# A new order and start of the attention head, GpSimd reciprocals, and a split end in a fused attention and two-MoE kernel

## The chip, the cores and the metric

The kernel runs on one core of one Trainium2 chip. The metric is the device time of one execution in microseconds (us). A core has TensorE (PE, with its weight loads PEld), VectorE (DVE), ScalarE (ACT), GpSimd (POOL) and SyncE (SP), which here issues DMAs. Each engine works through its own queue in order.

## The reference

Window attention (each token sees itself and the 63 before it) is followed by two pairs of dense layers: one with a squared ReLU, one with a rational function.

```python
B, H, S, D = 4, 8, 576, 64
scores = scale * np.matmul(q, k.transpose(0, 1, 3, 2))
mask = (rel >= 0) & (rel < 64)
scores = np.where(mask, scores, -1000000000.0)
attn = np.exp(scores - np.max(scores, axis=-1, keepdims=True))
attn = attn / (np.sum(attn, axis=-1, keepdims=True) + 1e-09)
x = np.matmul(attn, v)                      # to (2304, 512)
h = x @ w_in1; x = (np.maximum(h, 0) ** 2) @ w_out1          # d_ff 2048
h = x @ w_in2
g = (a0 + a1*h + a2*h**2 + a3*h**3) / (1 + |b0|*|h| + |b1|*h**2 + 1e-6)
out = g @ w_out2
```

All arrays are float32. The dense products are made of three products of rounded parts (high by high, high by low, low by high), so each operand is split into a high and a low part before it is used.

## The kernel before

The 2304 tokens are cut into 18 sub-blocks of 128 and five blocks of 512 or less. Attention of a sub-block `i` consists of slots: `q` and `k` (transpose on TensorE, copy out of PSUM to qT and kT), `s` (score products for two groups of 64 queries, `gl` 0 and 1, then `softmax`), `p` (transpose of the probabilities, one for each group, and a copy), `x` (product with v, then `split_x` into xh and xl). For sub-blocks 1 to 3 `y` makes a part of the product with v early. For sub-block 0, `Q`, `K` and `S` are halves of `q`, `k` and `s`, each for half of the heads.

Sub-blocks 0 to 3 (`i < NS0`) form the head: nothing dense can run before their x is there. The list `begin` (L1445) gives the order of their slots, and so the due time of each: n times 30000/32 for entry n. From then on the dense products `h` (L923 for the first one, L933 after it) and `acc` (L950) run, with the attention of later sub-blocks between them. Weights come as two-word numbers: a load, a decode (ScalarE L457, VectorE L459 and L462), a high part (ScalarE L492) and a low part (VectorE L493). At the end the second pair of layers runs (`product` L1301, `outs` L1336), and `evac2` copies the last rows out and stores them. The last 128 rows are made in two halves (L1322), copied (L1392) and stored (L1393) separately.

The order on every engine is fixed when the program is built. `Plan.run` is a list scheduler: it takes the item that can start first by the plan's own durations, at equal starts the one with the earliest due time, and each engine then runs its items in that order. A due time is carried back from user to producer: the user's due time, less the producer's duration, less 150 ns. A copy may name two engines ("act" and "dve"), and the plan picks one. Loads are items of a single DMA engine in the plan; a load of `size` bytes counts `size/360*slow` ns, and lands by the plan `LANDS` ns later, a list that is used up load by load. All of them are issued from SP (L345). PSUM has eight banks; the list `banks` (L569) gives the bank of each of the first slots.

`softmax` (L757): `top` on VectorE adds the mask and takes the row maximum (nm), `exp` on ScalarE gives the exponentials and their sums (su), `norm` on VectorE (L790, L791) makes the reciprocals of the sums (rs), and `mul` multiplies, in the head on GpSimd (L794), later on VectorE. There are two softmaxes in each sub-block, so eight in the head, each with four maxima, four exponentials, one `norm` and one `mul`. `warm_up` (L1437) is six products of `ident` by itself ahead of the first transposes; `ident` and `mask` are made by GpSimd at the start.

For sub-block 0 the first 64 queries have no earlier keys. The kernel before keeps their keys in columns 64 to 127 of the scores, masks columns 0 to 63, and loads the first 64 tokens of v once more to the upper 64 partitions (`load_v`, L423) so that the product with v can use rows 64 to 127.

Of the kernel before, what the change touches and what calls it, by code (L numbers as in the profile page):

```python
# [15 lines left out]
NEG = -1.0e30  # L16
# [139 lines left out]
def window_attention__moe_relu2__moe_rational_kernel(  # L156
# [54 lines left out]
    SMALL = [("cb", 2), ("coef", 6), ("na", 4), ("b1", 1), ("b0", 1)] + [(f"{x}{i}", 4) for x in ("nm", "su", "rs") for i in range(4)]  # L211
    TAGS = ([("ident", [128, 128], F32), ("mask", [128, 4 * W], F32)] +
            [(f"kT{i}", [128, HP, W + 128], F32) for i in range(2)] + [(x, [128, n], F32) for x, n in SMALL] +
            [("pad", [128, 208], F32)] + [("sm2", [128, 4, 128], F32)] +
# [122 lines left out]
    LANDS = [1500, 1800, 1900, 1800, 1700, 1600, 1500, 1400, 1300, 1200, 1350, 3050, 2650, 2700, 2450, 2650, 3000, 3000, 4300, 4000,  # L337
# [231 lines left out]
    banks = list([0, 1, 2, 3, 4, 5, 6, 7, 0, 1, 2, 3, 4, 6, 5, 7, 0, 1, 2, 3, 4, 5, 6, 7, 1, 0, 2, 3, 4, 5])  # L569
# [82 lines left out]
    def slot_half(nm, z, due):  # L652
        src = nat[nm, 0]
        if z == 0:
            t = buf(SM[0] if nm == "k" else QTP, [128, HP, 128])
            (kT if nm == "k" else qT)[0] = t
            ps = ps_buf()
            half[nm, "T"] = ps, halves(ps), t, halves(t)
        ps, phs, t, ths = half[nm, "T"]
# [7 lines left out]
        it = plan.add({"pe": 230}, tr, [half[nm][z]], [phs[z]], due)  # L667
        src.readers.append(it)
        ps.writers.append(it)
        it = plan.add({"act": act(256, True), "dve": dve(256)}, lambda e: (  # L670
            A.copy(out=t.t[:, c], in_=ps.t[:, c]) if e == "act" else V.tensor_copy(t.t[:, c], ps.t[:, c])),
            [phs[z]], [ths[z]])
        ps.readers.append(it)
        t.writers.append(it)

    def slot_S(z, due):
        if z == 0:
            half["s"] = [(b, halves(b)) for b in (ps_buf(), ps_buf())]
        ps = [b for b, _ in half["s"]]
        it = plan.add({"pe": 700}, lambda _: scores(0, ps, range(z * HP // 2, (z + 1) * HP // 2)),  # L680
                      [half[x, "T"][3][z] for x in "qk"], [b[z] for _, b in half["s"]], due)
# [875 lines left out]
```

## Time and profile before

| | us |
|---|---|
| median of 3 runs | 843.41 (843.02 to 844.32) |
| profiled execution | 843.76 |
| its span, first to last instruction | 841.8 |
| PE busy | 833.3 (99%) |
| DVE busy | 677.0 (80%) |
| ACT busy | 610.4 (73%) |
| POOL busy | 66.9 (8%) |

The shares of busy time are averages over stages with different limits. The start of the dense part is seen in the timeline of TensorE, and its end in that of all engines. In the rows below, a group names the line, the engine, the operation, out<-in by the program's names and shapes, and a count. An idle time stands with the event that ended it.

### The profile page before, as it was taken

The page shows a single profiled execution, that of the slowest core. Times are in us where ns is not written, and L with a number is a line of the kernel's source. Part 1 is how long each engine was busy: PE and PEld are TensorE (multiplying, and loading weights), DVE is VectorE, ACT ScalarE, POOL GpSimd, SP SyncE. Part 2 cuts the span into 40 slices and gives each one's busy share as a digit, 9 for nine tenths or more (in the row PEclk, how much of TensorE's full clock was granted, in tenths as well). Part 3 has the DMA queues.
Part 4 walks back from the last instruction along what each step waited for, and adds up shares of the span by engine and source line. Part 5 has one row for each costly group of instructions (what it writes and reads, how often), then busy time and mean ns, then how long its engine had stood idle before and what let it go on. Part 6 is the DMA issues. An engine that isn't in the chain of part 4 may idle for free.

```text
span 841.8 us, 15587 instructions
## 1 busy us (share of the span) xinstructions
PE 833.3 (99%) x5502; PEld 725.9 (86%) x5502; DVE 677.0 (80%) x1483; ACT 610.4 (73%) x1275; POOL 66.9 (8%) x124
## 2 busy tenths in 40 slices
PE   8999999999999999999999999999999999999998
PEld 7888888888888888888899999988999988999986
DVE  6999875866577778756464599999999999899993
ACT  6988864655465666545665898988898977989963
POOL 3100002224302222000000000000000000000000
PEclk9999999999999999999999999999999999999999
DMA  9987866998769988866699999784655772652011
GB/s 177 290 235 213 238 149 169 272 229 219 201 219 315 252 257 246 286 209 205 185 360 376 373 373 323 235 306 126 183 150 162 225 262 76 183 153 65 2 38 37
DMA packets 208605, 180.47 MB, mean 214 GB/s; under 512 B 97296, under 2 KB 161040, under 8 KB 208528
## 3 DMA queue, kind: packets, MB, share of 16 engines
q1 hardware_dynamic: 204368, 168.99, 67.1%
q0 software_dynamic: 4160, 10.49, 4.0%
q8 instruction: 43, 0.70, 0.4%
q14 instruction: 34, 0.28, 0.1%
HBM read 129.90 MB, written 53.74 MB: 218 GB/s over the span
## 4 chain that ended last, share of the span: by engine, by line
PE 93%; DMA 3%; SPq 2%; ACT 1%; DVE 0%; issue 0%; ACTq 0%
PE acc L950 23%; PE h L933 23%; PE acc L1336 12%; PE h L1336 8%; PE acc L1301 8%; PE t L1301 7%; PE h L1301 4%; PE t L1336 4%; SPq L345 2%; PE h L835 2%; DMA wih<-w2c_d 1%; PE t L743 1%; DMA xl<-in_moe_w_in_dram 1%; DMA xh<-x2s_d 1%; PE t L748 1%; PE t L826 0%
## 5 line engine op out<-in xcount | busy, mean ns | idle before, releaser
L950 PE MATMUL acc<-g,wo 128*128 128x512 f32 (+1 forms) x960 | 212.8, 370 | 0.0
L950 PEld LDWEIGHTS acc<-g,wo 128*128 128x128 f32 x960 | 167.4, 189 | 29.9 <-issue 0.2
L974 ACT ACTIVATE cvr<-h 128x512 f32<-128x512 f32 (+1 forms) x80 | 44.4, 554 | 109.8 <-PE h L933 105.3
L981 DVE TENSOR_TENSOR g<-cvr,g 128x512 fp32r<-128x512 f32 (+1 forms) x80 | 50.7, 634 | 55.5 <-ACT cvr L979 55.1
L933 PE MATMUL h<-xh,wx 128*128 128x512 f32 (+1 forms) x292 | 90.6, 370 | 0.0
L933 PE MATMUL h<-xh,wil 128*128 128x512 f32 (+1 forms) x180 | 66.3, 368 | 0.0
L933 PEld LDWEIGHTS h<-xh,wx 128*128 128x128 f32 x292 | 53.5, 189 | 9.1
L933 PE MATMUL h<-xh,wih 128*128 128x512 f32 (+1 forms) x160 | 59.5, 372 | 0.0
L933 PE MATMUL h<-xl,wih 128*128 128x512 f32 (+1 forms) x160 | 58.9, 368 | 0.0
L933 PE MATMUL h<-xl,wx 128*128 128x512 f32 (+1 forms) x156 | 57.4, 368 | 0.0
L1336 PE MATMUL acc<-wo,g 128*128 128x512 f32 x234 | 57.3, 391 | 0.0
L1336 PEld LDWEIGHTS acc<-wo,g 128*128 128x128 f32 x234 | 43.8, 188 | 8.8
L1336 PE MATMUL acc<-wo,cvr 128*128 128x512 f32 x198 | 48.7, 391 | 0.0
L976 ACT ACTIVATE g<-cvr 128x512 fp32r<-128x512 f32 (+1 forms) x80 | 47.0, 588 | 1.9
L786 ACT ACTIVATE sm<-sm,nm 128x128 f32<-128x128 f32 x112 | 43.7, 392 | 5.0 <-DVE nm L782 4.9
L345 POOL DMA_DIRECT2D sm<-p_d x80 | 44.5, 558 | 21.1 <-DMA p_d<-sm 13.8
L462 DVE SCALAR_TENSOR_TENSOR cvr<-cvr,raw 128x512 uint32<-128x512 uint32 x60 | 41.0, 685 | 5.1 <-ACT cvr L457 3.9
L1336 PEld LDWEIGHTS acc<-wo,cvr 128*128 128x128 f32 x198 | 37.0, 188 | 7.3
L457 ACT ACTIVATE cvr<-raw 128x512 f32<-128x512 f32 x60 | 39.8, 668 | 2.6 <-DMA raw<-in_moe_w_in_dram 2.3
L1336 PE MATMUL h<-wo,cvr 128*128 128x512 f32 x153 | 38.9, 390 | 0.0
L933 PEld LDWEIGHTS h<-xh,wil 128*128 128x128 f32 x180 | 33.9, 189 | 5.6
L933 PEld LDWEIGHTS h<-xh,wih 128*128 128x128 f32 x160 | 30.2, 189 | 5.1
(303 smaller groups left out, 1957.7 us busy)
## 6 DMA issues: line engine op xcount, KB each, us to landing
wil<-w2c_d SPq DMA_DIRECT2D x72, 256.0 KB, 3.4
wih<-w2c_d SPq DMA_DIRECT2D x64, 256.0 KB, 3.2
raw<-in_moe_w_out_dram SPq DMA_DIRECT2D x30, 512.0 KB, 5.6
raw<-in_moe_w_in_dram SPq DMA_DIRECT2D x16, 512.0 KB, 5.6
w_d<-raw SPq DMA_DIRECT2D x16, 512.0 KB, 4.6
wo<-w_d SPq DMA_DIRECT2D x16, 512.0 KB, 6.6
raw<-in_moe_w_in_dram SPq DMA_DIRECT2D x28, 256.0 KB, 4.4
w2c_d<-raw SPq DMA_DIRECT2D x16, 448.0 KB, 3.7
```

The costliest lines, as they stand in the source:

```text
L345: (P if own else nc.sync).dma_start(out=o, in_=i)
L457: plan.add({"act": act(DM)}, lambda e: A.activation(out=t.t, in_=raw.t.bitcast(F32)[:, :, 1], func=ACTF.Prelu, scale=2.0 ** -112, alpha=2. ...
L462: plan.add({"dve": dve(DM)}, lambda e: V.scalar_tensor_tensor(out=u(t), in0=u(t), scalar=3, in1=raw.t[:, :, 0], op0=ALU.logical_shift_left ...
L786: A.activation(out=head(c), in_=head(c), func=ACTF.Exp, scale=-1.0, bias=nm.t[:, c:c + 1], accum_out=su.t[:, c:c + 1])
L835: T.matmul(out=ps.t[e * 64:(e + 1) * 64, hp, gl * W:(gl + 1) * W], lhsT=v.t[rows, 2 * hp + e, :], rhs=(pT[i, gl].t[:, (e ^ gl) * 2:(e ^ gl ...
L933: T.matmul(out=v4(hp.t, n), lhsT=w.t[:, (c ^ 2) * 128:((c ^ 2) + 1) * 128], rhs=x.t[:, :n // 128, c, :], start=(c == 0 and z == 0), stop=( ...
L950: T.matmul(out=v4(acc[l, bi, m].t, n), lhsT=w.t[:, m, :], rhs=y.t[:, :n // 128, :], start=st, stop=en)
L974: plan.add({"act": act(n, True)}, lambda e: A.activation(out=r.t[:, :n], in_=hp.t[:, :n], func=ACTF.Relu), [hp], [r])
L976: plan.add({"act": act(n)}, lambda e: A.activation(out=gh.t[:, :nq], in_=v4(r.t, n), func=ACTF.Square), [r], [gh])
L981: plan.add({"dve": dve(n)}, lambda e: V.tensor_tensor(out=gl.t[:, :nq], in0=v4(r.t, n), in1=gh.t[:, :nq].bitcast(F32), op=ALU.subtract), [ ...
L1301: T.matmul(out=v4(ps.t, TW), lhsT=wb.t[:, (2 * (1 - z) + c) * 128:(2 * (1 - z) + c + 1) * 128], rhs=xb.t[:, :, 2 * y + c, :], start=k in ( ...
L1336: T.matmul(out=v4(ac.t, DM), lhsT=y.t[:, m, :], rhs=w.t, start=j == 0 and z == 0, stop=j == end_ and z == 2)
```

## The change

- `norm` of the first four sub-blocks runs on GpSimd: the sum plus 1e-9, then that to the power of minus one, with a constant tile `minus`. The plan counts 200 ns for the two; `mul` follows on GpSimd as before.
- The halves of sub-block 0 (`K`, `Q`, `S`) have PSUM banks of their own instead of sharing.
- The first 64 queries keep their keys in columns 0 to 63 of the scores. The mask gets one more part of 64 columns, and the second load of the first 64 tokens of v falls away.
- The warm-up is five products of a zero tile that VectorE sets; two more follow the first transposes of q.
- `begin`, `banks` and `LANDS` are new lists.
- Of the last 128 rows, the second half is copied by VectorE and its store issued from ScalarE's queue.

```diff
-            [("pad", [128, 208], F32)] + [("sm2", [128, 4, 128], F32)] +
+            [("pad", [128, 136], F32)] + [("sm2", [128, 4, 128], F32)] +
...
+    minus = sb.tile([128, 1], F32, tag="minus", name="minus")
+    P.memset(minus, -1.0)
+    zeros = sb.tile([128, 128], F32, tag="ld", name="zeros")
+    V.memset(zeros, 0.0)
     make_identity(nc, ident)
-    mask = sb.tile([128, 4 * W], F32, tag="mask", name="mask")
+    mask = sb.tile([128, 5 * W], F32, tag="mask", name="mask")
     P.memset(mask, 0.0)
-    P.memset(mask[:, 0:W], NEG)
+    for s in (0, 4 * W):
+        P.memset(mask[:, s:s + W], NEG)
...
-    LANDS = [1500, 1800, 1900, 1800, 1700, 1600, 1500, 1400, 1300, 1200, 1350, 3050, 2650, 2700, 2450, 2650, 3000, 3000, 4300, 4000,
+    LANDS = [1500, 1800, 1900, 1800, 1700, 1600, 1500, 1400, 1300, 1200, 1300, 1500, 1700, 2000, 2200, 2500, 2600, 4000, 3800,
              3900, 3900, 3900, 3500]
...
             if i < NS0:
-                if gl or not i:
-                    t = nat["v", g] = nat_buf(2 + gl, i)
-                    o, n = (0, 128) if gl else (W, W)
-                    load(t, lambda t=t, o=o, n=n: [(t.t[o:o + n], v[0, :, i * 128:i * 128 + n, :].rearrange(
-                        "h p d -> p h d"))], n << 11, 1.8)
+                if gl:
+                    t = nat["v", g] = nat_buf(3, i)
+                    load(t, lambda t=t: [(t.t, v[0, :, i * 128:i * 128 + 128, :].rearrange("h p d -> p h d"))], 1 << 18, 1.8)
...
-    banks = list([0, 1, 2, 3, 4, 5, 6, 7, 0, 1, 2, 3, 4, 6, 5, 7, 0, 1, 2, 3, 4, 5, 6, 7, 1, 0, 2, 3, 4, 5])
+    banks = list([3, 5, 6, 7, 3, 1, 6, 4, 2, 1, 0, 7, 1, 6, 5, 2, 0, 7, 5, 2, 4, 6, 0, 3, 0, 3, 4, 1, 3, 4, 2, 4, 5, 1])
...
             for x in range(c.start, c.stop):
                 T.transpose(ps.t[:, x, :], s[:, x * 128:(x + 1) * 128], ident)
+            if (nm, z) == ("q", 0):
+                warm_up(2)
...
     def slot_S(z, due):
-        if z == 0:
-            half["s"] = [(b, halves(b)) for b in (ps_buf(), ps_buf())]
-        ps = [b for b, _ in half["s"]]
+        ps = half["s", z] = [ps_buf(), ps_buf()]
...
-                    for z, x in enumerate(two[::-1] if 0 < i < NS0 else two):
+                    for z, x in enumerate(two[::-1] if i < NS0 else two):
...
-        m0 = 0 if (2 * i + gl) % GPB == 0 else 2 * W if gl or i >= NS0 else W
+        m0 = 3 * W if 2 * i + gl == 0 else 0 if (2 * i + gl) % GPB == 0 else 2 * W if gl or i >= NS0 else W
...
         def norm(_):
+            if i < NS0:
+                P.tensor_scalar(out=rs.t, in0=su.t, scalar1=1e-9, scalar2=None, op0=ALU.add)
+                P.tensor_tensor(out=rs.t, in0=rs.t, in1=minus.to_broadcast([128, 4]), op=ALU.pow)
+                return
             V.tensor_scalar(out=rs.t, in0=su.t, scalar1=1e-9, scalar2=None, op0=ALU.add)
             V.reciprocal(out=rs.t, in_=rs.t)
...
-        plan.add({"dve": 350}, norm, [su], [rs])
+        plan.add({"pool": 200} if i < NS0 else {"dve": 350}, norm, [su], [rs])
         plan.add({"pool": 1150} if i < NS0 else {"dve": 690}, mul, [rs, t], [t])
...
-                values(i, gl, ps, vg[gl], hp, slice(0 if i or gl else W, 128), True, True)
+                values(i, gl, ps, vg[gl], hp, slice(0, 128 if i or gl else W), True, True)
...
-                plan.add({"act": 334}, lambda _, o=o, cs=cs: A.copy(out=o.t, in_=c.t[:, cs]), [last[z]], [o])
-                plan.add({"dma": 364}, lambda _, o=o, cs=cs: nc.sync.dma_start(out=rows[:, cs], in_=o.t), [o], due=finish)
+                plan.add({"dve": 350} if z else {"act": 334}, lambda _, o=o, z=z, cs=cs: (
+                    V.tensor_copy(o.t, c.t[:, cs]) if z else A.copy(out=o.t, in_=c.t[:, cs])), [last[z]], [o])
+                plan.add({"dma": 364}, lambda _, o=o, z=z, cs=cs: (A if z else nc.sync).dma_start(
+                    out=rows[:, cs], in_=o.t), [o], due=finish)
...
-    def warm_up(_):
-        for _ in range(6):
-            T.matmul(out=warm.t[:, :128], lhsT=ident, rhs=ident, start=True, stop=True)
-
-    plan.add({"pe": 1200}, warm_up, [], [warm], 0)
+    def warm_up(n):
+        for _ in range(n):
+            T.matmul(out=warm.t[:, :128], lhsT=zeros, rhs=zeros, start=True, stop=True)
+
+    plan.add({"pe": 3050}, lambda _: warm_up(5), [], [warm], 0)
...
-    begin = ("Q0,K0,K1,Q1,S0,S1,k1,q1,k2,q2,s1,p00,p01,k3,s2,q3,x0,p10,y1,p11,s3,x1,p20,y2,p21,k4,q4,x2,p30,y3,p31,x3").split(",")
+    begin = ("K0,Q0,Q1,S0,K1,k1,S1,q1,k2,s1,k3,p01,p00,q2,s2,q3,s3,p10,x0,y1,p11,p20,x1,p30,y2,p21,q4,y3,x2,k4,p31,x3").split(",")
```

## Rows read from the trace of the kernel before

**Rows 1.** The page, part 1: busy time, share of the span, instructions.

```profile
PE 833.3 (99%) x5502; PEld 725.9 (86%) x5502; DVE 677.0 (80%) x1483; ACT 610.4 (73%) x1275; POOL 66.9 (8%) x124
```

**Rows 2.** TensorE's waits, 30 to 838 us: line, waited for, total, times, longest.

```profile
PE h L1301 <- ACT h L1308: 0.3, 1, 0.3
```

**Rows 3.** The chain of waits, 0 to 60 us: start, length, what.

```profile
21.45 5.98 DMA xl<-in_moe_w_in_dram
...
30.04 3.07 PE h L923 x24
```

**Rows 4.** By stretch: length, busy times, granted clock, DMA share, GB/s.

```profile
20.00:25.00 5.00, 4.47 (x73) 3.79 (x70) 4.61 (x27) 5.00 (x23) 2.29 (x4) 1.00 1.00 277
```

**Rows 5.** ScalarE's timeline: start, length, instruction, [idle before, releaser].

```profile
7.42 0.41 ACT L786 ACTIVATE wih<-wih,nm 128x128 f32<-128x128 f32 x1
...
24.11 0.19 ACT L786 ACTIVATION_READ_ACCUMULATOR wil<-wil,nm 128x1 f32 x1
...
25.62 0.70 ACT L457 ACTIVATE cvr<-xh 128x512 f32<-128x512 f32 x1
```

**Rows 6.** ScalarE's groups, 0 to 30 us: count, busy, mean ns, idle, releasers.

```profile
L786 ACT ACTIVATE wih<-wih,nm 128x128 f32<-128x128 f32 x16 | 6.3, 395 | 1.3 <-DVE nm L782 1.3
L786 ACT ACTIVATE wil<-wil,nm 128x128 f32<-128x128 f32 x16 | 6.3, 394 | 0.3 <-DVE nm L782 0.3
```

**Rows 7.** The timeline of VectorE in the head.

```profile
10.75 0.73 DVE L790 TENSOR_SCALAR rs<-su 128x4 f32<-128x4 f32 x1
```

**Rows 8.** VectorE's groups by line, 0 to 30 us.

```profile
L790 DVE TENSOR_SCALAR rs<-su 128x4 f32<-128x4 f32 x8 | 1.9, 236 | 0.2 <-ACT wil L786 0.2
...
L791 DVE RECIPROCAL rs<-rs 128x4 f32<-128x4 f32 x8 | 1.4, 178 | 0.3
...
L671 DVE COPY sm<-h 128x256 f32<-128x256 f32 x1 | 0.4, 424 | 5.2 <-PE h L665 5.2
```

**Rows 9.** GpSimd's groups by line, 0 to 30 us.

```profile
L794 POOL TENSOR_TENSOR wil<-wil,rs 128x512 f32<-128x512 f32 x4 | 4.4, 1096 | 3.4 <-DVE rs L791 2.2 <-ACT wih L786 1.2
L794 POOL TENSOR_TENSOR wih<-wih,rs 128x512 f32<-128x512 f32 x4 | 4.2, 1040 | 11.1 <-DVE rs L791 10.2 <-ACT wil L786 0.9
...
L240 POOL MEMSET cb<- 128x1 f32 x1 | 0.1, 98 | 0.1
```

**Rows 10.** GpSimd's first product and the reciprocal that releases it: two timelines.

```profile
10.08 0.18 DVE L791 RECIPROCAL rs<-rs 128x4 f32<-128x4 f32 x1
...
10.41 1.04 POOL L794 TENSOR_TENSOR wih<-wih,rs 128x512 f32<-128x512 f32 x1 [7.24 <-DVE rs L791]
```

**Rows 11.** The timeline of TensorE in the head.

```profile
1.36 2.93 PE L1439 MATMUL acc<-ident 128*128 128x128 f32 x12 [1.36 <-POOL ident masks.py:199]
...
5.75 0.28 PE L754 MATMUL t<-sm,qT 64*64 64x64 f32 x2 [0.61 <-DVE sm L671]
```

**Rows 12.** DMA issues, 0 to 40 us: queue, count, size, us to landing.

```profile
xh<-in_moe_w_in_dram SPq DMA_DIRECT2D x2, 256.0 KB, 3.3
...
wil<-in_q_dram SPq DMA_DIRECT2D x2, 128.0 KB, 2.7
```

**Rows 13.** SP's queue in the head: start, time held, issue.

```profile
0.74 0.44 SPq L345 DMA_DIRECT2D wil<-in_q_dram  x1
...
8.73 4.12 SPq L345 DMA_DIRECT2D wo<-in_v_dram  x4
12.89 3.69 SPq L345 DMA_DIRECT2D ld<-in_k_dram  x2
...
19.13 1.14 SPq L345 DMA_DIRECT2D xh<-in_moe_w_in_dram  x2
```

**Rows 14.** The timeline of all engines at the end.

```profile
838.08 0.65 ACT L1392 COPY pT<-h 128x256 f32<-128x256 f32 x2 [0.80 <-PE h L1322]
838.48 0.81 SPq L1393 DMA_DIRECT2D out_dram<-pT  x2
```

**Rows 15.** DMA issues, 834 to 842 us.

```profile
out_dram<-pT SPq DMA_DIRECT2D x2, 128.0 KB, 1.8
```

More of the change, by code (lines that the diff above doesn't have):

```diff
@@ L204, in window_attention__moe_relu2__moe_rational_kernel @@
     plan = Plan()
-    SMALL = [("cb", 2), ("coef", 6), ("na", 4), ("b1", 1), ("b0", 1)] + [(f"{x}{i}", 4) for x in ("nm", "su", "rs") for i in range(4)]
-    TAGS = ([("ident", [128, 128], F32), ("mask", [128, 4 * W], F32)] +
+    SMALL = [("minus", 1), ("cb", 2), ("coef", 6), ("na", 4), ("b1", 1), ("b0", 1)] + [(f"{x}{i}", 4) for x in ("nm", "su", "rs") for i in range(4)]
+    TAGS = ([("ident", [128, 128], F32), ("mask", [128, 5 * W], F32)] +
             [(f"kT{i}", [128, HP, W + 128], F32) for i in range(2)] + [(x, [128, n], F32) for x, n in SMALL] +
-            [("pad", [128, 208], F32)] + [("sm2", [128, 4, 128], F32)] +
+            [("pad", [128, 136], F32)] + [("sm2", [128, 4, 128], F32)] +
             [(f"wx{i}", [128, 3, DM], F32R) for i in range(5)] +
@@ L656, in slot_half @@
             (kT if nm == "k" else qT)[0] = t
-            ps = ps_buf()
-            half[nm, "T"] = ps, halves(ps), t, halves(t)
-        ps, phs, t, ths = half[nm, "T"]
+            half[nm, "T"] = t, halves(t)
+        t, ths = half[nm, "T"]
+        ps = ps_buf()
         c = slice(z * HP // 2, (z + 1) * HP // 2)
@@ L665, in tr @@
                 T.transpose(ps.t[:, x, :], s[:, x * 128:(x + 1) * 128], ident)
-        it = plan.add({"pe": 230}, tr, [half[nm][z]], [phs[z]], due)
+            if (nm, z) == ("q", 0):
+                warm_up(2)
+        it = plan.add({"pe": 860 if (nm, z) == ("q", 0) else 430}, tr, [half[nm][z]], [ps], due)
         src.readers.append(it)
-        ps.writers.append(it)
         it = plan.add({"act": act(256, True), "dve": dve(256)}, lambda e: (
             A.copy(out=t.t[:, c], in_=ps.t[:, c]) if e == "act" else V.tensor_copy(t.t[:, c], ps.t[:, c])),
-            [phs[z]], [ths[z]])
-        ps.readers.append(it)
+            [ps], [ths[z]])
         t.writers.append(it)
     def slot_S(z, due):
-        if z == 0:
-            half["s"] = [(b, halves(b)) for b in (ps_buf(), ps_buf())]
-        ps = [b for b, _ in half["s"]]
+        ps = half["s", z] = [ps_buf(), ps_buf()]
         it = plan.add({"pe": 700}, lambda _: scores(0, ps, range(z * HP // 2, (z + 1) * HP // 2)),
-                      [half[x, "T"][3][z] for x in "qk"], [b[z] for _, b in half["s"]], due)
+                      [half[x, "T"][1][z] for x in "qk"], ps, due)
         for x in "qk":
-            half[x, "T"][2].readers.append(it)
-        for b in ps:
-            b.writers.append(it)
+            half[x, "T"][0].readers.append(it)
         if z:
             for gl in range(2):
-                softmax(0, gl, *half["s"][gl])
+                softmax(0, gl, None, [half["s", y][gl] for y in range(2)])
     def slot_sx(i, due, lag=1):
@@ L781, in top @@
         def top(c):
-            V.tensor_tensor_reduce(out=head(c), in0=keys(ps.t[:, c, :]), in1=keys(mask[:, m0:m0 + 2 * W]), scale=-scale,
+            V.tensor_tensor_reduce(out=head(c), in0=keys((phs[c * 2 // HP] if phs else ps).t[:, c, :]), in1=keys(mask[:, m0:m0 + 2 * W]), scale=-scale,
                                    scalar=-NEG, op0=ALU.add, op1=ALU.min, accum_out=nm.t[:, c:c + 1])
@@ L870, in slot_x @@
         ps = ps or ps_buf()
-        vg = [nat["v", 2 * i + gl] for gl in range(2)]
+        vg = [nat["v", 2 * i + gl] for gl in range(2)] if i else [nat["v", 1]] * 2
         def mm(_):
```

2 lines of the change are left out of this document (removed).

## The prediction, made from these rows alone

> **What bounds the kernel now.** I read the page's busy times first, then TensorE's own waits by stretch, then the chain of waits of the first 60 us, then both ends. TensorE is busy 833.3 of 841.8 us [rows 1], and between 30 and 838 us it waits for another engine just once, 0.3 us [rows 2]. The amount of that work is not changed. So the time is: the head up to the first dense product, a middle that TensorE fills, and the tail after its last product. Only head and tail can give anything, unless the change opens a new gap in the middle.
>
> The head ends where h (L923) starts, at 30.04 us [rows 3]. Between 20 and 25 us VectorE is busy 4.61 and ScalarE 5.00 of 5 us, GpSimd 2.29: the first two are full and GpSimd is half idle [rows 4]. The long series is the 32 exponentials of sub-blocks 0 to 3 on ScalarE: first at 7.42, last sum read at 24.11 + 0.19 = 24.30, so 16.9 us [rows 5]. 12.6 us of it is the exponentials' own work (6.3 + 6.3), 1.6 us (1.3 + 0.3) is idle time that ended with a row maximum (nm) from VectorE [rows 6]; the other 2.7 us, by subtraction, are copies and small gaps. Why VectorE was late with a maximum is in its timeline: a 128x4 addition for the reciprocal (L790) holds it 0.73 us at 10.75, against a mean of 0.24, because it waits for its last sum; the maxima of sub-block 1 queue behind it [rows 7, 8]. After the last exponential the chain goes through the landing of the second w_in block (27.43, 5.98 us after its second issue), ScalarE's decode of it, the last copy before x3, x3 itself and h [rows 3].
>
> **The change, part by part.**
>
> *Reciprocals to GpSimd.* VectorE loses eight additions and eight reciprocals: 1.9 + 1.4 = 3.3 us of busy time at 236 and 178 ns each, the waiting in one of them included [rows 8]. What that is worth on the path is not 3.3 us but what the exponentials waited for VectorE, 1.6 us [rows 6]: I take 1.6. Ends: 0, if other VectorE work stands in the same places; and 3.5, if besides the 1.6 most of the 2.7 us of copies leaves ScalarE for the freed VectorE (the code lets a plan choose the engine of these copies).
>
> GpSimd gains eight additions and eight powers on 128x4. The trace has no power on GpSimd. The nearest rows below are a memset of 128x1, 98 ns, and above a product of 128x512, 1040 ns [rows 9]; so the pair lies between 0.2 and 2.1 us, and a power made of many steps could lie higher. I take 0.35 us, near the lower row because four columns are 128 times fewer than 512. GpSimd idles 3.4 + 11.1 us around its eight products, 7.24 us of that ahead of the first [rows 9, 10]; so 7.3 us (3.4 + 11.1 - 7.24) lie between the products, and 8 x 0.35 = 2.8 us fit there. Queued behind each new pair is the product of the same softmax and then the next one's; TensorE's transposes of p wait for those. Against that, the hand-over from VectorE falls away: the sum goes to an idle GpSimd instead of into VectorE's queue. I cost the latency at nothing; if the cover is gone, it is the pair's price less 0.35 on every softmax.
>
> On GpSimd's first use of an operation: its first product starts at 10.41, released by a reciprocal that began at 10.08 and took 0.18, so no load of code shows there [rows 10]. The Trainium skill (GPSIMD Engine Reference, section 2.1, Instruction dispatch) says that the first call of a freshly loaded kernel pays about 6 us (5.95) without a visible instruction; the multiply's row shows none of it, and no run so far shows a power. By that figure, an estimate, the sum below would lose 6 - (7.3 - 2.8) = 1.5 us and come to 842.5. The sum itself takes no such hold-up; rival E prices it from rows.
>
> *Start.* Warm-up now needs ident from GpSimd, starts at 1.36, lasts 2.93, and the first score product starts at 5.75 [rows 11]. A zero tile from VectorE lets it start before ident is ready, and five products instead of six take 2.93 x 5/6 = 2.4 us. The first 128 KB of q take 2.7 us from their issue at 0.74 [rows 12, 13], so they are there at about 3.4, and TensorE was still warming up then. K0, Q0 and Q1 follow with two more warm-up products, 2 x 0.49, after Q0. I take scores 0.5 us earlier; ends 0 and 0.75 (4.29, the end of warm-up, less 3.4, is 0.9, and the two products take some of it). GpSimd's longer mask and VectorE's memset lie before 5 us, where both are idle: nothing.
>
> *Loads.* One of 128 KB (v for the first 64 tokens) goes. SP took 4.12 us for it and three loads of 256 KB [rows 13], so it counts 4.12/7 = 0.6 us and one of 256 KB 1.2. The new order also swaps issues in SP's queue. By the due times in the code (30000/32 = 937.5 per step; 1311 + 150 off for a 256 KB load) v of sub-block 3 is due at 27 x 937.5 - 1461 = 23.9 where it was 29 x 937.5 - 1461 = 25.7; k of sub-block 4 goes from 22.0 to 25.7; the first w_in block, counted back from h, stays at 25.6. So w_in 0 passes k4, whose two pieces held SP 3.69 us, and is passed by v of sub-block 3 (1.2 us). Its two issues took 1.14 us from 19.13 on [rows 13], landing 3.3 us after the issue [rows 12], at about 23; it should land 0.6 to 3 us earlier. ScalarE took it up only at 25.62 [rows 5], so it isn't late even if the head is 2 us shorter. The second w_in block now has k4 ahead of it; without the 128 KB I expect it 0.6 us earlier, at 26.8. In the kernel before ScalarE's queue stood still for it just ahead of the last copy for x3. In the new one the copy is ready earlier and can go first. I credit 0; ends -1.5 (it stands still again) and +0.6.
>
> *Separate PSUM banks for the halves, new bank order.* The halves take more turns of the eight banks in the same time. None of TensorE's long waits in the head is for a bank, so I cost it at nothing; the cover is that a bank's copy is done before its next turn, and if it isn't, one wait as long as a copy (0.4 us for 128x256 [rows 8]) stands ahead of a slot.
>
> *Last rows.* Both last copies are on ScalarE from 838.08, and both issues on SP, 0.81 us from 838.48 [rows 14]; the landing takes 1.8 [rows 15]. A copy of 128x256 on VectorE took 424 ns [rows 8], ScalarE's two 0.65 together, so the second half is copied by 838.55 and issued from ScalarE at once, instead of about 838.9 (838.48 + 0.81/2). Gain 0.3. ScalarE issues no DMA in the kernel before; the nearest rows are SP's 0.81 for two and 3.69 for the pair of k4 [rows 13, 14]. Ends: +0.4, and -1.7 if the issue costs half of 3.69 more.
>
> *Sum.* Profiled execution 843.76 (841.8 span and 1.96 around it): 0.5 + 1.6 + 0 + 0.3 = 2.4 us less, 841.4. The median of the runs is 0.35 lower, so 841.0.
>
> **What is late next.** With the exponentials 2.1 us earlier, their end is 22.2; then come, as before, some 5.7 us of copies, x3 and the decode of w_in 0, so h starts near 27.9. If VectorE has time in hand, the next wall is a landing.
>
> **The rivals.**
>
> A, the forecast: 841.0, with 839.0 to 841.7 as its own range.
>
> B, a transfer takes the place of the wait. If w_in 1 stands in ScalarE's queue ahead of what x3 needs, h follows its landing by 30.04 - 27.43 = 2.6 us: 26.8 + 2.6 = 29.4, a gain of 0.6, with the tail 0.9: 842.5. The like holds if h starts early and waits again at the second or third w_in block, where both engines are full. For it: the chain of the kernel before passes exactly there [rows 3]. Against it: the copy for x3 has the earlier due time.
>
> C, the change doesn't do what it says: VectorE's freed time is filled by copies and the exponentials stay where they were. Tail alone: 843.1. For it: both engines are full [rows 4]. Against it: the work of the two together shrinks by 3.3 us.
>
> D, GpSimd becomes the bound; slower. From the first four sums (7.42 + 4 x 0.395 = 9.0) to the last product in the kernel before (24.30 + 0.24 + 0.18 + 1.10 = 25.8 [rows 5, 8, 9]) there are 16.8 us for eight softmaxes, 2.1 us each; product and hand-over take 1.2. So from a pair price of 0.9 us on the head gets longer than before. At 1.5 us it ends 8 x 0.6 = 4.8 us later: 843.4 + 4.8 - 0.3 = 847.9; at 2.1, the upper row, 852.7. The plan orders TensorE's queue by 0.2 us for the pair, so scores can queue behind transposes that wait. Against it: four columns only.
>
> E, the first power is held up once. GpSimd can lose 7.3 - 2.8 = 4.5 us between its products before the last one is late. Bounds from rows: no hold-up, as at the multiply's first call; and 7.24 us, the longest stretch in which GpSimd does nothing [rows 10]. So the loss is 0 to 2.7 us; half of it, 1.4, gives 842.4. Against it: the multiply's row. The page named above speaks for it.
>
> **How the numbers follow.** Chances: A 0.60, B 0.19, C 0.06, E 0.04, D 0.11. 0.2% of 843.41 is 1.7 us, about what a measurement can tell from no change: below 841.7 faster, above 845.1 slower. Faster is A, 0.60; same is B, C and E, 0.29; slower D, 0.11. The range goes from 839.0 (2 us more than the forecast, when copies leave ScalarE too) to 843.9 (C with a small loss at either end); D and a few hundredths below 839.0 stay outside.
>
> **What will show it.** Right: the first score product before 5.5; the maxima of sub-block 1 before 11; the idle time of the exponentials for nm under 0.5 us; the last exponential near 22; h near 28; TensorE without a wait over 0.5 us behind it; the pair on GpSimd under 0.5 us; the last issue at 838.6 less the head's gain. Wrong: GpSimd without gaps between 9 and 26 (D); a first power that starts late (E); ScalarE idle until w_in 1 lands, or a wait of TensorE in the first 20 us of the dense part (B); exponentials that end at 24 as before (C).

## The result: slower, by 6 us

The changed kernel takes 849.43 us in the median of 6 runs (848.47 to 852.60), the kernel before 843.21 us beside it; the ratio is 1.0072, with a 95% interval of 1.006 to 1.0085. The forecast of 841.0 us and its range, which ended at 843.9, were wrong, and so was the sign. The profiled execution of the changed kernel is one of 848.47 us with a span of 846.7 us, 4.9 us more than before; it is the fastest of the six.

In the changed kernel lines have moved a little: the maxima are L781, the exponentials L785, addition and power L790 and L791, the product on GpSimd L797, the transposes of p L827, the product with v L836, the first h L924, the first out product L951. First the page, part 1 (busy time, share of the span, instructions):

```profile
PE 836.1 (99%) x5504; PEld 727.5 (86%) x5504; DVE 676.8 (80%) x1471; ACT 609.9 (72%) x1272; POOL 77.4 (9%) x142
```

Against [rows 1] GpSimd has 10.5 us more, at an unchanged VectorE. Its groups over the whole span (count, busy time, mean ns of one, idle time ahead of them):

```profile
L791 POOL TENSOR_TENSOR rs<-rs,minus 128x4 f32<-128x4 f32 x8 | 8.5, 1061 | 0.7
L797 POOL TENSOR_TENSOR wih<-wih,rs 128x512 f32<-128x512 f32 x4 | 4.4, 1095 | 0.3
L797 POOL TENSOR_TENSOR wil<-wil,rs 128x512 f32<-128x512 f32 x4 | 4.2, 1040 | 0.3
L790 POOL TENSOR_SCALAR rs<-su 128x4 f32<-128x4 f32 x8 | 1.8, 228 | 8.2 <-ACT wil L785 7.3 <-ACT wih L785 0.4
```

The power on 128x4 takes as long as the product on 128x512: 1061 ns against 1040 to 1095. The products' idle time, 3.4 + 11.1 us in [rows 9], is 0.6 us now: GpSimd works without a gap but for one of 0.4 us at 21 us, where it waits for a sum. Its timeline (start, length, instruction, idle time before and its releaser) shows the period; after these lines it goes on in the same way to the last product:

```profile
10.69 0.23 POOL L790 TENSOR_SCALAR rs<-su 128x4 f32<-128x4 f32 x1 [7.34 <-ACT wil L785]
11.00 1.04 POOL L791 TENSOR_TENSOR rs<-rs,minus 128x4 f32<-128x4 f32 x1
12.12 1.04 POOL L797 TENSOR_TENSOR wil<-wil,rs 128x512 f32<-128x512 f32 x1
13.25 0.23 POOL L790 TENSOR_SCALAR rs<-su 128x4 f32<-128x4 f32 x1
...
30.68 1.04 POOL L797 TENSOR_TENSOR wil<-wil,rs 128x512 f32<-128x512 f32 x1
```

One softmax takes GpSimd 13.25 - 10.69 = 2.56 us. The last product ends at 31.72; in the kernel before the eight products began 2.07 us apart on average and the last ended at 26.20. Who waited for this is read in TensorE's waits over the whole span (line, waited for, total, times, longest):

```profile
PE h L827 <- POOL wih L797: 2.3, 1, 2.3
PE t L827 <- POOL wih L797: 1.9, 1, 1.9
...
PE acc L827 <- POOL wil L797: 0.8, 1, 0.8
PE h L1302 <- ACT h L1309: 0.3, 1, 0.3
```

The transposes of the probabilities wait 5.0 us for GpSimd's products; 0.3 us behind the head is the same as in [rows 2]. The chain of waits (start, length, what) goes through the same engine, and h, which [rows 3] have at 30.04, starts at 34.83:

```profile
26.60 1.23 POOL rs L791
27.90 1.27 POOL wih L797
29.22 0.66 PE h L827 x4
...
34.83 1.26 PE h L924 x9
```

So 4.8 of the 4.9 us stand ahead of the first h. From the first out product (L950 before, L951 after) to the end both kernels take the same time: 841.8 - 36.96 = 804.8 and 846.7 - 41.74 = 805.0. Of the experiments below e1, e2, e4, e6, e8, e9 and e11 give 804.8 to 805.1 here, so they are read by what they do to the head. In e7, e10 and e12 it is 805.4 to 805.6, because the first out product stands alone there ahead of a wait; e3 has 806.0 (its first out product waits in the same way, 0.2 us) and e5, with another order of the dense part, 804.0. A single profile has a noise of its own: e6, whose head is that of the kernel before, had the first out product at 37.81 in an execution of 844.53 us, 0.85 us later than in the profile of before.

One more thing is in the windows (stretch, length, busy time with count of PE, PEld, DVE, ACT and POOL, granted clock, DMA share, GB/s):

```profile
10.00:15.00 5.00, 3.02 (x60) 2.22 (x60) 3.66 (x19) 4.38 (x22) 3.90 (x6) 1.00 1.23 215
15.00:20.00 5.00, 4.22 (x66) 3.50 (x68) 2.52 (x13) 2.17 (x11) 4.51 (x7) 0.73 1.05 221
20.00:25.00 5.00, 4.88 (x122) 4.32 (x120) 4.10 (x23) 4.33 (x22) 4.30 (x6) 0.93 1.01 216
25.00:30.00 5.00, 2.61 (x53) 2.16 (x48) 3.84 (x10) 2.63 (x11) 4.51 (x7) 1.00 1.03 324
```

Behind the wait of 1.9 us that ended at 15.78 TensorE's granted clock is 0.73 and then 0.93 on average (0.50, its lower level of 1.2 GHz, throughout the stretch from 18 to 20 us); in the kernel before it is 1.00, the level of 2.4 GHz, from 20 to 25 us [rows 4]. Not every such wait lowers it: after the longer one of 2.3 us, which ended at 29.22, it stays 1.00 up to 38 us. The mean granted clock of a whole execution goes with its time. The six runs of the changed kernel took 848.47 and 848.89 us at a mean clock of 0.998, 849.11, 849.75 and 849.99 at 0.996, and 852.60 at 0.992. VectorE and ScalarE are no longer full from 20 to 25 us: 4.10 and 4.33 against 4.61 and 5.00.

### The profile page after: what moved, and what is told of

It reads as the page before. It is cut to its first block, busy times and chain, and to the rows that moved or that the text cites. A ratio compares the mean times of both kernels' runs of the same rounds, so it can differ in the third digit from the quotient of the medians.

```text
span 846.7 us, 15577 instructions
## 1 busy us (share of the span) xinstructions
PE 836.1 (99%) x5504; PEld 727.5 (86%) x5504; DVE 676.8 (80%) x1471; ACT 609.9 (72%) x1272; POOL 77.4 (9%) x142
## 4 chain that ended last, share of the span: by engine, by line
PE 96%; ACT 2%; POOL 1%; DVE 1%; DMA 0%; issue 0%; SPq 0%; ACTq 0%
PE acc L951 24%; PE h L934 23%; PE acc L1337 12%; PE h L1337 8%; PE acc L1302 8%; PE t L1302 7%; PE h L1302 4%; PE t L1337 4%; PE h L836 2%; PE t L742 1%; PE t L747 1%; PE t L827 1%; POOL rs L791 0%; PE t L617 0%; PE h L924 0%; DMA wil<-in_q_dram 0%
## 5 line engine op out<-in xcount | busy, mean ns | idle before, releaser
L951 PE MATMUL acc<-g,wo 128*128 128x512 f32 (+1 forms) x960 | 212.5, 370 | 0.0
L951 PEld LDWEIGHTS acc<-g,wo 128*128 128x128 f32 x960 | 167.5, 189 | 30.1 <-issue 0.2
L785 ACT ACTIVATE sm<-sm,nm 128x128 f32<-128x128 f32 x112 | 43.6, 391 | 6.8 <-DVE nm L781 6.8
```

The source lines that it names most:

```text
L785: A.activation(out=head(c), in_=head(c), func=ACTF.Exp, scale=-1.0, bias=nm.t[:, c:c + 1], accum_out=su.t[:, c:c + 1])
L951: T.matmul(out=v4(acc[l, bi, m].t, n), lhsT=w.t[:, m, :], rhs=y.t[:, :n // 128, :], start=st, stop=en)
```

## The experiments

Each was compared with runs of the kernel before on the same chip. The theory after the result was that the power's price makes GpSimd the bound (rival D); its rivals were the new order of slots with its changed start, the plan's wrong price for the pair, and the rest of the change. A second question was where the forecast gain would have gone with a cheap reciprocal.

**e1, the same order with a cheap operation.**

```diff
-                P.tensor_tensor(out=rs.t, in0=rs.t, in1=minus.to_broadcast([128, 4]), op=ALU.pow)
+                P.tensor_tensor(out=rs.t, in0=rs.t, in1=minus.to_broadcast([128, 4]), op=ALU.mult)
```

> The changed kernel with a product (by minus one) in place of the power, so the probabilities come out scaled; every engine keeps its order of instructions. Theory, the power's price: in the changed kernel the power took 1.04 us on 128x4, addition, power and product 2.55 us from one softmax to the next, and eight of them filled GpSimd from 10.7 to 31.7 us. With a product of about 0.25 us the same order fits its plan: h starts at 28 to 30 instead of 34.8, median 841 to 843.5. Rival, the order itself: banks, loads and the order of TensorE's queue hold the head: h stays after 33, median above 847.

Measured: 843.36 us (10 runs), ratio 0.9999, interval 0.999 to 1.0009. e1's group of this operation on GpSimd, 8 to 36 us:

```profile
L791 POOL TENSOR_TENSOR rs<-rs,minus 128x4 f32<-128x4 f32 x8 | 1.6, 203 | 0.7
```

And its chain of waits ahead of h:

```profile
17.73 6.71 DMA ld<-in_k_dram
...
24.57 0.63 PE acc L640 x4
...
29.71 3.07 PE h L924 x24
```

With 203 ns in place of 1061 and every instruction in its place the whole loss is gone: the power's price is the cause of it. The pair still takes 10.74 - 10.15 = 0.59 us in e1, gaps included. But the forecast's gain isn't there either. The last exponential of the head ends 1.05 us earlier (it starts at 22.77, before at 23.82), yet h starts at 29.71, only 0.33 us earlier (less than the 0.85 us by which two profiles of the same head differ), since the transposes of k4 now wait for their load.

**e2, the norms on VectorE, all else as changed.**

```diff
-            if i < NS0:
-                P.tensor_scalar(out=rs.t, in0=su.t, scalar1=1e-9, scalar2=None, op0=ALU.add)
-                P.tensor_tensor(out=rs.t, in0=rs.t, in1=minus.to_broadcast([128, 4]), op=ALU.pow)
-                return
...
-        plan.add({"pool": 200} if i < NS0 else {"dve": 350}, norm, [su], [rs])
+        plan.add({"dve": 350}, norm, [su], [rs])
```

> The changed kernel with addition and reciprocal back on VectorE at the plan's old 350 ns; all else of the change stays, and the plan draws a new order. If the power is the whole loss: 841 to 843.4, at or under the kernel before. If the late start (scores at 6.37 instead of 5.75 us) and the new lists cost by themselves: 844 to 846.

Measured: 846.84 us (6 runs, three of them near 845.3 and three near 848.6, so the median lies between two groups), ratio 1.0044, interval 1.0026 to 1.0063; the profiled execution took 845.30 us, with a span of 843.2. The two groups go with the granted clock: the three runs of 845.27 to 845.30 have a mean of 0.999, the three of 848.37 to 848.89 one of 0.996. The first group lies in the range of the second expectation, the other above both. So the rest of the change, with the norms on VectorE, is a loss of about 2 us by itself, and of more where the clock falls. e8 and e9 go on from here.

**e3, the power alone**, in the kernel before: the four lines of `norm`, the tile `minus` and the price of 200 ns, and nothing else.

```diff
+            if i < NS0:
+                P.tensor_scalar(out=rs.t, in0=su.t, scalar1=1e-9, scalar2=None, op0=ALU.add)
+                P.tensor_tensor(out=rs.t, in0=rs.t, in1=minus.to_broadcast([128, 4]), op=ALU.pow)
+                return
...
-        plan.add({"dve": 350}, norm, [su], [rs])
+        plan.add({"pool": 200} if i < NS0 else {"dve": 350}, norm, [su], [rs])
```

> The kernel before with nothing but the reciprocal as a power on GpSimd, planned at 200 ns. If the power's price sets the loss: eight times (2.55 - 2.1) us more in the head, 846 to 850. If it takes the changed order to make it late: within 1 us of 843.2.

Measured: 848.95 us (4 runs), ratio 1.0064, interval 1.0049 to 1.0079. TensorE's waits from 8 to 60 us, the longest three:

```profile
PE h L832 <- POOL wih L800: 2.0, 2, 1.0
PE acc L832 <- POOL wih L800: 1.3, 1, 1.3
PE h L832 <- POOL wil L800: 1.1, 2, 0.7
```

One part of the change, put into the kernel before, brings nearly the whole loss, with the same waits for GpSimd's products (the plan draws the order of the engines anew for it). All four runs have a mean granted clock of 1.000, so this loss of 5.6 us is there without a fall of the clock. The power is enough by itself, and the new order doesn't mend it.

**e4, the price by itself:** seven operations on idle GpSimd at the start of the kernel before.

```diff
+    for n in (4, 1, 8, 16, 32):
+        P.tensor_tensor(out=pry[:, :n], in0=prx[:, :n], in1=minus.to_broadcast([128, n]), op=ALU.pow)
+    P.tensor_tensor(out=pry[:, :4], in0=prx[:, :4], in1=minus.to_broadcast([128, 4]), op=ALU.mult)
+    P.tensor_scalar(out=pry[:, :4], in0=prx[:, :4], scalar1=1e-9, scalar2=None, op0=ALU.add)
```

> The kernel before with a row of idle GpSimd work between 3.3 and 10 us: powers on 128 x 4, 1, 8, 16 and 32, a product and an addition on 128x4, to read their spans. If the power pays by the element (0.2 us and more for each column): 1 column under 0.5 us, 8 about 1.8, 32 about 6. If it pays a fixed price of a call: all near 1 us. Product and addition on four columns: 0.2 to 0.3.

This kernel was run once (849.78 us), and only its rows are read. GpSimd's groups, 3 to 16 us:

```profile
L248 POOL TENSOR_TENSOR pry<-prx,minus 128x32 f32<-128x32 f32 x1 | 5.4, 5417 | 0.1
L248 POOL TENSOR_TENSOR pry<-prx,minus 128x16 f32<-128x16 f32 x1 | 2.9, 2896 | 0.1
L248 POOL TENSOR_TENSOR pry<-prx,minus 128x8 f32<-128x8 f32 x1 | 1.6, 1643 | 0.1
L248 POOL TENSOR_TENSOR pry<-prx,minus 128x4 f32<-128x4 f32 x1 | 1.0, 1040 | 0.1
...
L248 POOL TENSOR_TENSOR pry<-prx,minus 128x1 f32<-128x1 f32 x1 | 0.6, 566 | 0.1
L250 POOL TENSOR_SCALAR pry<-prx 128x4 f32<-128x4 f32 x1 | 0.2, 229 | 0.1
L249 POOL TENSOR_TENSOR pry<-prx,minus 128x4 f32<-128x4 f32 x1 | 0.2, 202 | 0.1
```

From 1 to 32 columns the power grows by (5417 - 566)/31 = 156 ns a column. The product grows by (1040 - 202)/508 = 1.6 ns a column from 128x4 to 128x512 [rows 9]. A column of power costs as much as some 95 columns of product, so "128 times fewer columns" was no argument for a low price.

**e5, the true price in the plan.**

```diff
-        plan.add({"pool": 200} if i < NS0 else {"dve": 350}, norm, [su], [rs])
+        plan.add({"pool": 1350} if i < NS0 else {"dve": 350}, norm, [su], [rs])
```

> The changed kernel, the power kept, but the plan told 1350 ns for addition and power (the product-for-power run read 1.04 + 0.23 us and gaps) instead of 200, so TensorE's queue is ordered for the real price. If the loss is GpSimd's fill alone: eight times 2.55 us stay, h at 33 to 35, 847 to 850. If a good part is TensorE waiting in a wrong order, with the clock that falls after such a wait: h at 31 to 33 and 844 to 847.

Measured: 850.70 us (4 runs, 848.71 to 852.58), ratio 1.0088, interval 1.0068 to 1.0108. The two runs at a mean clock of 0.999 took 848.71 and 849.60, those at 0.994 851.81 and 852.58; the last is the profiled one, and its h starts at 37.67, later than either expectation had it. At 0.999 that is about what the changed kernel takes at 0.998: a plan that knows the price finds no better order for this list of slots, and the wrong price isn't the loss.

**e6, the split end alone**, in the kernel before.

```diff
-                plan.add({"act": 334}, lambda _, o=o, cs=cs: A.copy(out=o.t, in_=c.t[:, cs]), [last[z]], [o])
-                plan.add({"dma": 364}, lambda _, o=o, cs=cs: nc.sync.dma_start(out=rows[:, cs], in_=o.t), [o], due=finish)
+                plan.add({"dve": 350} if z else {"act": 334}, lambda _, o=o, z=z, cs=cs: (
+                    V.tensor_copy(o.t, c.t[:, cs]) if z else A.copy(out=o.t, in_=c.t[:, cs])), [last[z]], [o])
+                plan.add({"dma": 364}, lambda _, o=o, z=z, cs=cs: (A if z else nc.sync).dma_start(
+                    out=rows[:, cs], in_=o.t), [o], due=finish)
```

> The kernel before with the split end alone (second half copied by VectorE, stored from ScalarE's queue); every other instruction stays in its place. The prediction's 0.3 us: from the end of TensorE's last product to the end of the span 3.75 us go to 3.4 or 3.5. The rival, read from the changed kernel, where VectorE's copy began only when ScalarE's was done: 3.7 to 3.9, no gain. In the runs nothing that can be measured.

Measured: 843.49 us (10 runs), ratio 1.0005, interval 0.9995 to 1.0014. The end of its timeline:

```profile
838.92 0.37 ACT L1393 COPY pT<-h 128x256 f32<-128x256 f32 x1 [0.80 <-PE h L1322]
...
839.32 0.42 DVE L1393 COPY pT<-h 128x256 f32<-128x256 f32 x1 [7.71 <-ACT pT L1393]
839.78 0.37 ACTq L1394 DMA_DIRECT2D out_dram<-pT  x1
```

VectorE's copy starts only when ScalarE's has ended, and the bracket names that copy. So the two halves follow one another as before; the last store is issued 839.78 + 0.37 - 838.92 = 1.23 us after the first copy starts, in [rows 14] 838.48 + 0.81 - 838.08 = 1.21. The changed kernel shows the same wait, 7.71 us behind ACT pT.

**e7, e1 with k4's load earlier**, to take away the wait that e1 showed.

```diff
-                                          for o, n, bi, s in toks(i * 128, 128)], 1 << 18, 1.8, lag=late(i, 4000))
+                                          for o, n, bi, s in toks(i * 128, 128)], 1 << 18, 1.8, lag=late(i, 4000),
+                 due=22000 if (i, nm) == (NS0, "k") else None)
```

> The run with a product in place of the power, and k of sub-block 4 due at 22.0 us again, so that its load goes ahead of w_in. In that run the chain into h went through k4's landing (24.4 us), 0.7 us of wait on TensorE just ahead of the last values. If the landing is the next wall: h at 27.5 to 28.8, 841.5 to 842.5. If another wait stands right behind it: h at 29.3 to 30, within 0.5 us of 843.4.

Measured: 843.62 us (10 runs), ratio 1.0006, interval 0.9996 to 1.0015. h starts at 28.68, 1.29 us earlier than before (29.97 in the same view, [rows 3] have 30.04 in the chain), and the span is 841.6, as in e1. So h came as early as the first expectation had it, and the time as the second. TensorE's wait in the dense opening, from its waits of 8 to 45 us:

```profile
PE acc L952 <- DVE g L983: 0.4, 1, 0.4
```

And, in VectorE's timeline, the product that ends it:

```profile
36.15 0.69 DVE L983 TENSOR_TENSOR g<-cvr,g 128x512 fp32r<-128x512 f32 x1
```

The out products of the opening, of which only the first gets through (35.97), wait until 36.89 for g. A head that is 1.29 us shorter ends at the next wall, with 0.2 us left over in the span.

**e8, e2 with k4's load earlier.**

```diff
+                 due=22000 if (i, nm) == (NS0, "k") else None)
```

> Reciprocals on VectorE in the changed kernel (845.3 in three runs of six, about 848.5 in the other three) and k4's load early as in the run beside it. If k4 was the hold-up: 842 to 844. If it was the order of VectorE's queue (additions that wait for their sums, copies behind them): 845 to 847 as before.

Measured: 844.73 us (10 runs), ratio 1.0013, interval 1.0004 to 1.0023; h at 30.72. That is between the two expectations, and 0.6 us less than e2's runs at a clock of 0.999. The longest waits of TensorE in the head are 0.8 us for GpSimd's product and 0.8 and 0.7 us for ScalarE's copies of the probabilities.

**e9, e8 without the two products after the first transposes of q.**

```diff
-            if (nm, z) == ("q", 0):
-                warm_up(2)
...
-        it = plan.add({"pe": 860 if (nm, z) == ("q", 0) else 430}, tr, [half[nm][z]], [ps], due)
+        it = plan.add({"pe": 430}, tr, [half[nm][z]], [ps], due)
```

> The kernel of e8_vector_k4_early (norm on VectorE, k4's load earlier) with one edit more: the two warm-up products that the change put between the halves of Q's transposes are taken out, and the planned price of that transpose goes back from 860 to 430. Nothing is left out of the result. My theory is that the start step had the wrong sign: those products stand ahead of the first score and not beside a wait. It expects the first score near 5.1 to 5.5 us instead of 5.93, and, because the next walls of the opening (the norms on VectorE, the dense part's ScalarE and VectorE queues) aren't touched, a time of 844.0 to 844.8 against 844.73. The rival, that the start sets the end one for one, expects 843.9 or less; the other rival, that the extra products only fill a wait for Q's landing, expects the first score at 5.8 to 6.0 as before.

Measured: 843.87 us (10 runs), ratio 1.0007, interval 0.9998 to 1.0016; first score at 4.92 (5.65 to 6.37 in the profiles of all kernels with the changed start), h at 29.56, span 841.4. The two profiles speak against my expectation that the start would do little to the time, and for the rival's "one for one": the first score comes 6.10 - 4.92 = 1.18 us earlier than in e8, h 1.16, the span 1.2. The medians are 0.86 us apart, but the intervals of the two ratios overlap, so the runs alone don't show it. The price in the plan fell as well and with it the order changed somewhat; how much of the 0.86 belongs to that isn't told apart.

**e10, e7 with light exponentials in sub-block 4**, to ask what holds g in e7.

```diff
         def exp(c):
+            if i == NS0:
+                A.activation(out=su.t[:, c:c + 1], in_=nm.t[:, c:c + 1], func=ACTF.Exp, scale=0.0)
+                return
...
-            V.tensor_scalar(out=rs.t, in0=su.t, scalar1=1e-9, scalar2=None, op0=ALU.add)
+            V.tensor_scalar(out=rs.t, in0=su.t, scalar1=1e37 if i == NS0 else 1e-9, scalar2=None, op0=ALU.add)
```

> The kernel of e7_product_k4_early (multiplication by minus one in place of the power, k4's load earlier) in which ScalarE's exponentials of sub-block 4 act on one column in place of 128, so the probabilities of that sub-block are left out of the result; all engines keep their order. It asks what holds the first output product at 36.6 to 36.9 us in e7 although the first gate product came at 28.7. My theory is ScalarE's queue in the opening of the dense part: six of those exponentials, some 0.3 us shorter each, stand on it between 31 and 36.5. It expects the first output product 0.5 to 1.5 us earlier, a span of 840.1 to 841.1 and a time of 842.1 to 843.1. The rival, that VectorE's or a load's chain holds it, expects a span of 841.4 to 841.9 and a time of 843.3 to 843.7, with ScalarE idle in that stretch for the difference.

Measured: 843.38 us (10 runs), span 841.6. My theory (ScalarE's queue) fell. VectorE's product of g, L986 in e10, starts at 36.19 against 36.15, and ScalarE only waits longer for a maximum:

```profile
31.35 0.20 ACT L787 ACTIVATE su<-nm 128x1 f32<-128x1 f32 x1 [1.05 <-DVE nm L782]
...
36.19 0.68 DVE L986 TENSOR_TENSOR g<-cvr,g 128x512 fp32r<-128x512 f32 x1
```

**e12, e7 with sub-block 4's multiplications on GpSimd**, so that VectorE has 0.69 us less ahead of g.

```diff
-            (P if e == "pool" else V).tensor_tensor(out=full(), in0=full(), in1=sums(), op=ALU.mult)
+            (P if e == "pool" or i == NS0 else V).tensor_tensor(out=full(), in0=full(), in1=sums(), op=ALU.mult)
```

> The kernel of e7_product_k4_early (a multiplication by minus one in place of the power, so the probabilities of sub-blocks 0 to 3 are left scaled; k4's load earlier) in which the two multiplications of sub-block 4's probabilities by their reciprocals are put on GpSimd, which is idle by then; every other instruction of every engine keeps its place. With ScalarE's queue ruled out by e10_product_light_exp, my theory is now VectorE's queue: it is busy for 4.9 of each 5 us from 20 to 40 us there, and TensorE's wait for the gate g (0.45 us in e7, 0.32 us in e10) ends with VectorE's product of it. The multiplication ahead of g takes 0.69 us, so the theory expects g 0.4 to 0.7 us earlier, that wait at under 0.1 us, a span of 840.9 to 841.4 against 841.6 and a time of 842.9 to 843.5. The rival, that TensorE's own order or a load holds the stretch, expects the wait to come back in front of another instruction and the span at 841.5 to 841.8; a second rival, that GpSimd's product (about 1.04 us) makes the transposes of sub-block 4's probabilities late, expects a new wait of 0.3 us or more ahead of them.

Measured: 843.71 us (10 runs), span 841.6. This theory (VectorE's queue alone) fell too: g starts at 36.16, and VectorE waits for ScalarE's high part of the weights instead:

```profile
33.48 0.91 DVE L497 TENSOR_TENSOR wo<-cvr,wo 128x512 fp32r<-128x512 f32 x1 [0.66 <-ACT wo L496]
36.16 0.68 DVE L983 TENSOR_TENSOR g<-cvr,g 128x512 fp32r<-128x512 f32 x1
```

Work taken from one engine's queue didn't move g, because that engine then waited for the other. But neither run touched the decodes of weights that stand on the way from h to g. In all three kernels ScalarE's first step on h (L976 in e7) waits for h itself, 0.2 to 0.5 us, and g follows the start of h by 7.3 to 7.6 us (36.15 - 28.68 = 7.47 in e7), in the kernel before by 35.91 - 29.97 = 5.94. In e7 two of them are on ScalarE and then one on VectorE just ahead of g, as its chain of waits shows:

```profile
32.36 0.66 ACT cvr L461
...
34.94 0.58 ACT cvr L461
...
35.54 0.04 DVE cvr L466
```

In the kernel before, VectorE's timeline has its decode (L462) behind g (L981):

```profile
35.91 0.69 DVE L981 TENSOR_TENSOR g<-cvr,g 128x512 fp32r<-128x512 f32 x1
36.52 0.69 DVE L462 SCALAR_TENSOR_TENSOR cvr<-cvr,raw 128x512 uint32<-128x512 uint32 x1
```

So the order that the plan gave to the opening is a rival for this last wall; whether another order lets the shorter head through wasn't tried.

**e11, the waits filled**: the changed kernel with six products of `ident` ahead of the transposes of p00 and p30.

```diff
         def tr(_):
+            for _ in range(6 if (i, n) in ((0, 0), (3, 0)) else 0):
+                T.matmul(out=ps.t[:, 0, :], lhsT=ident, rhs=ident, start=True, stop=True)
             for c in range(4):
```

> The changed kernel with six products of the identity with itself ahead of the transposes of the probabilities of the first and of the fourth sub-block, written into the bank that those transposes then overwrite: TensorE does something in the two waits for GpSimd. Nothing is left out of the result. If the granted clock that fell to 0.66 to 0.91 between 16 and 24 us is part of the loss, that clock is 0.95 or more here and the time is 847.0 to 848.6, with a narrower spread than the 848.5 to 852.6 of the changed kernel. The rival, that GpSimd's 1.35 us per pair is the whole of it and the clock only follows, expects 848.8 to 849.9, whatever the clock does in that stretch; a third outcome, that the added products themselves delay the transposes, would be over 850.

Measured: 847.86 us (4 runs, 847.70 to 848.18), ratio 1.005, interval 1.0033 to 1.0067. The windows from 15 to 25 us, as above:

```profile
15.00:20.00 5.00, 4.57 (x113) 3.81 (x117) 3.28 (x19) 2.90 (x14) 4.51 (x7) 1.00 0.97 238
20.00:25.00 5.00, 4.33 (x115) 3.74 (x105) 4.26 (x21) 4.45 (x22) 4.51 (x7) 1.00 1.04 226
```

The clock stays at 1.00, the median is 1.6 us lower than the changed kernel's, and the spread is 0.5 us instead of 4.1. With the waits filled the clock didn't fall, and the fallen clock is a part of the loss that was measured, and the groups of runs in e2 and e5 go the same way; the larger part is there without it (e3). The median is from other runs on another occasion, so 1.6 us is rough. In the two profiled executions the spans differ by 0.8 us, 0.5 of which is there at GpSimd's first addition already (10.22 against 10.69).

## Why the prediction was wrong, step by step

**The step that failed is the price of the pair,** "0.35 us, near the lower row because four columns are 128 times fewer than 512". Addition, power and the two gaps behind them take 12.12 - 10.69 = 1.43 us. The bounds, 0.2 and 2.1, held it; the choice between them went by size alone, and the operation was a different one from those in both rows. The cover that hid it went with it: 8 x 1.43 = 11.4 us against the 7.3 us that lay between the products.

**Rival D is what happened,** with its chance put at 0.11. Its mechanism holds: a turning point where GpSimd fills a period of 2.1 us, and behind it a loss of the excess on every softmax. Its formula with the measured period in place of the 2.1 us gives 843.4 + 8 x (2.56 - 2.1) - 0.3 = 846.8; the profiled execution has 848.47. What is missing is the point it counts from: it let the first four sums be there at 9.0, while they end at 9.83 + 0.78 = 10.61 in the changed kernel's chain. The first exponential starts at 7.90 instead of 7.42, and the four of the first softmax don't follow one another: an exponential of the other softmax (8.69) and a copy of q stand between them in ScalarE's timeline.

```profile
9.24 0.59 ACT L622 COPY qT<-h 128x512 f32<-128x512 f32 x1
```

846.8 + 1.6 = 848.4, close to the profiled execution; the median lies 1.0 us above it, where the granted clock is lower.

**The gain of 1.6 us from VectorE's relief** was partly there and led nowhere. With the cheap operation (e1) the exponentials end 1.05 us earlier. They still waited 1.8 us in all, where [rows 6] have 1.6: 0.7 for the very first maximum, and 1.0 in one wait for GpSimd's norm, which ScalarE's timeline of e1 shows.

```profile
15.87 0.40 ACT L785 ACTIVATE wih<-wih,nm 128x128 f32<-128x128 f32 x1 [1.03 <-POOL rs L791]
```

So the waits for VectorE inside the series did go, and the norm on its new engine brought most of the idle time back, a wait that the sum had not counted. The long addition at 10.75, which the prediction put down to its last sum, is not explained by it: ScalarE had read that sum by 10.42 + 0.19 = 10.61, and what held the addition stays open. And what is late next, which the prediction left open with "the next wall is a landing", is two walls: the landing of k4 (e1) and, behind it, the way from h to g over ScalarE and VectorE in the opening of the dense part (e7, e10, e12). That is rival B's kind of wait, at another load and further on; so with a reciprocal as cheap as a product, too, the result would have been "same", as e1's 0.9999 says. The head's gain was summed as if nothing stood behind h.

**Start** brought no gain. I expected the first score 0.5 us before 5.75 [rows 11]; it is at 6.37 here and at 5.65 to 6.37 in the nine profiles with this start:

```profile
3.34 0.65 PE L668 MATMUL h<-ident,wih 128*128 128x128 f32 x2
4.04 0.69 PE L668 MATMUL acc<-ident,wil 128*128 128x128 f32 x2
4.53 1.06 PE L1442 MATMUL acc<-zeros 128*128 128x128 f32 x4
5.38 0.63 PE L668 MATMUL acc<-ident,wil 128*128 128x128 f32 x2
...
6.37 0.38 PE L753 MATMUL acc<-sm,qT 64*64 64x64 f32 x2
```

The transposes do start earlier (3.34, before at 4.08), and the first ones of q are done at about 4.7. But the two extra products (four instructions, L1442) lie between them and the second ones of q and hold TensorE for 0.85 us of the chain (4.74 to 5.59), and K1 (5.81) has also come ahead of the first score, which the prediction had not counted. In e9, without the extra products, the first score is at 4.92.

**Loads** came in part as predicted. The first w_in block is issued at 15.06 instead of 19.13 [rows 13] and lands in 5.2 us, so at about 20.3; no wait of the changed kernel is for it. That k4 would be the late one, I had not seen: it was moved back in SP's queue behind w_in 0, was issued at 16.76, and in e1 it is the wall.

**Banks** show no cost: none of TensorE's waits above is for a copy out of a bank of the halves. **Last rows:** the term of 0.3 us was 0 (e6), because the copies of the two halves don't run beside one another. The price of an issue on ScalarE, 0.37 us, was on the cheap side of its bounds.

**Rival E** fell: the first power starts 0.08 us after its addition and takes 1.04 us, as the others do. The hold-up of about 6 us that the Trainium skill gives for the first call of a freshly loaded kernel (GPSIMD Engine Reference, section 2.1, Instruction dispatch) isn't to be seen in this trace or in e4's first power (1040 ns). **Rivals A and C** fell with the result.

Of the things that would show it: the signs of D, GpSimd without gaps from 9 to 26, came from 10.69 to 31.72, with the one gap of 0.4 us. The maxima of sub-block 1 come at 11.14 instead of 11.61, where under 11 was the mark, and the last exponential of the head starts at 26.51 instead of 23.82.

None of the versions that keep all of the computation beats the kernel before; the nearest are e6 at 1.0005, e9 at 1.0007 and e8 at 1.0013 of it.

## What to carry to other kernels

An operation that the trace has never shown on an engine is priced by measuring it at two sizes, not by its size against another operation's; where only bounds are at hand and one mechanism turns within them, its chance is the share of the bounds beyond the turning point (here 2.1 - 0.9 of 2.1 - 0.2, over a half), not a tenth. And before a gain at one wall is summed, ask which load and which queue stand right behind it: here a head shorter by 1.29 us gave 0.2.

## What the runs showed of the hardware

- GpSimd's power: 566, 1040, 1643, 2896 and 5417 ns on 1, 4, 8, 16 and 32 columns; the product on 4 columns 202 ns, on 512 1040.
- A copy on VectorE from one half of a PSUM bank began only when ScalarE's copy from the other half had ended (e6: 838.92 + 0.37, then 839.32), though each writes a tile of its own; whether the bank or the tile they share is the reason wasn't tried.
- After a wait of 1.9 us TensorE's granted clock was lower between 16 and 22 us (0.82, 0.50 and 0.83 in stretches of 2 us), after a later one of 2.3 us in the same execution it stayed 1.00. With products in both waits it was 1.00 from 10 to 32 us, and the times varied by 0.5 instead of 4.1 us (e11).
- Executions of the same program differed in mean granted clock, and in time with it: 845.27 to 845.30 us at 0.999 and 848.37 to 848.89 at 0.996 (e2).
